# Pooled attention and a top-1 mixture of experts: other key ranges for V's chunks, and low weight halves on another engine

## The chip, the cores and the metric

The kernel runs on one core of a Trainium2 chip. The core has a matrix engine (TensorE, in the profile PE, with its weight loads shown apart as PEld), a vector engine (VectorE, DVE), a scalar engine (ScalarE, ACT), GpSimd (POOL), SyncE (SP), which here only issues transfers, and 16 DMA engines. The metric is the time of the program on the device in microseconds (us), the median of a few runs; lower is better. The profile is of one further execution.

## The reference

Attention over pooled keys and values, and then a mixture of experts in which each token goes to one expert:

```python
# q, k, v: [8 batches, 8 heads, 576 tokens, 64]; pool = 8, so Sp = 72 pooled keys per head
k_p = k.reshape(B, H, Sp, pool, D).mean(axis=3)
v_p = v.reshape(B, H, Sp, pool, D).mean(axis=3)
scores = scale * np.matmul(q, k_p.transpose(0, 1, 3, 2))
attn = softmax(scores)                               # with + 1e-9 in the denominator
attn_out = np.matmul(attn, v_p)
x = attn_out.transpose(0, 2, 1, 3).reshape(4608, 512)
logits = x @ w_gate                                  # 8 experts
e = argmax(logits); gate_w = softmax(logits)[e]
out = gate_w * (relu(x @ w1[e]) @ w2[e])             # w1: 512 x 1024, w2: 1024 x 512 per expert
```

All data are float32.

## The kernel before

There are two stages. The first, up to about 200 us, is attention with the routing of its tokens; the second runs blocks of up to 256 tokens of one expert through that expert's two weight matrices.

**Attention.** The work is cut into 36 *units* of 128 tokens: four full units for each batch, and one unit for each pair of batches that holds the last 64 tokens of both (the *pair units*). One turn of the loop at line 937 does unit i. In each turn it emits, in this order: the pieces of GpSimd's work that are put down for this unit at position "q"; `u_pt(i)`, five transposes of the unit's unnormalised attention weights on TensorE and their copy to SBUF on ScalarE (line 494); half the scores of a later unit (`g_s`, line 468); transposes of later queries (`g_qt`, line 445); row minima on VectorE (`g_min`, line 478) and exponentials on ScalarE (`g_exp`, line 485); `u_pv(i)`, the matmuls with V (line 519, for pair units 514); small steps of the routing of earlier tokens (`fill`); the work put down at "dve3"; the transfers put down at "sp"; another half of scores; and `u_nrm(i)`, which normalises what `u_pv` left (lines 549 to 551). Each engine takes its instructions in this order and waits for the others by semaphores. `put(i, position, f)` is how work is assigned to a unit by hand.

`u_pv` writes to one PSUM tile `po`, of which there is one. So the V matmuls of unit i + 1 wait until line 551 of unit i has read it. Its matmuls are float32, and each is two instructions on TensorE.

**V in chunks.** The 576 pooled keys of a batch (8 heads of 72) lie on 128 partitions as five chunks c. `HS[c]` is the first head that chunk c touches, and `VB` holds for each chunk three masked copies of V, one for each head slot, with 8 columns of the gate's logits and a column of ones, 73 columns in all (`CW`). `SLOTS[c]` says which slots are multiplied. The chunks begin at keys 0, 128, 256, 384 and 512. Heads 0 to 3 lie in one PSUM bank and 4 to 7 in the next, so a chunk across this border takes two matmuls. In all a full unit has six matmuls of 2, 3, 1, 2, 3 and 1 heads: 12 heads, 876 columns.

**Pooling.** Groups of 8 tokens of K and V are added up by three additions of halves. For batch 0 VectorE does it (`pool_now`), and for the others GpSimd (`pool`, lines 327, 329 and 330), one K or V in two units, from `POOLAT[b]` on; batch 7 ends in unit 23. There are three buffers `kv`, so a transfer of K or V waits until GpSimd has read the one three before it. `masked` (line 406) writes pooled V into `VB`.

**K's half.** `v_act` appends to `moves` a copy of 64 partitions of pooled K from one half of `BD` to the other; line 968 issues it on SyncE's queue, where all loads are issued too.

**Weights.** The first expert's weights (float32) are loaded by four transfers of 1 MB (`wload`) and split each into two float16 halves: the high half on ScalarE (`wsplit`, "h", line 111), then the low half, what is left over. There are eight parts j. The low half of j = 0, 2, 5, 6, 7 is made on GpSimd by two instructions on a whole part (lines 118 and 119, "p"), and of j = 1, 3, 4 on VectorE in four pieces of 256 columns, in four units one after another (`lsplit`, line 804). `on_beat` makes such an instruction of GpSimd wait for the latest reciprocal of line 550.

**Routing.** After each group of four units a chain of small VectorE instructions (lines 593 to 649, among them 600, 606 and 615) finds each token's expert; TensorE ranks tokens (line 624) when line 615 is done, and GpSimd scatters the rows to DRAM (line 653). In units 33 to 35 TensorE already begins with the first expert's block (`up_early`, lines 924 to 926), and GpSimd prepares its tokens in unit 30 (`first_block`, lines 838 and 839).

Of the kernel before, what the change touches and what calls it, by code (L numbers as in the profile page):

```python
# [17 lines left out]
POOL = 8  # L18
# [5 lines left out]
UPAT = (33, 34, 35)  # L24
HS = (0, 1, 3, 5, 5)
SLOTS = ((0, 2), (0, 3), (0, 3), (0, 3), (2, 3))


@with_exitstack
def kernel(  # L30
# [110 lines left out]
    for c in range(5):  # L141
        nc.gpsimd.iota(rows[:, c, :], pattern=[[-KP, 3]], base=128 * c - KP * HS[c], channel_multiplier=1,
                       allow_small_or_imprecise_dtypes=True)
# [97 lines left out]
    def load_kv(b, src):  # L241
        dst = kv[(2 * b + (src is vf)) % 3]
        nc.sync.dma_start(dst[0:64, 4, :], src[b, 512:576, :])
        step = 2 if b == 0 else 4
        for c in range(4 - step, -1, -step):
            nc.sync.dma_start(dst[:, c:c + step, :],
                              src[b, 128 * c:128 * (c + step), :].rearrange("(c p) x -> p c x", p=128))
# [24 lines left out]
    nc.vector.memset(kv[0][64:128, 4, :], 0.0)  # L272
    for i in range(1, 3):
        nc.gpsimd.memset(kv[i][64:128, 4, :], 0.0)
    nc.vector.memset(BD[0], 0.0)
# [55 lines left out]

    def pool_now(src, dst, part):
        p1 = pbig[:, 0:1280].rearrange("p (c x) -> p c x", c=5)
        p2 = pbig[:, 1280:1920].rearrange("p (c x) -> p c x", c=5)
        c = (slice(2, 5), slice(0, 2))[part]
        nc.vector.tensor_tensor(p1[:, c], src[:, c, 0:4 * D], src[:, c, 4 * D:], op=OP.add)
        nc.vector.tensor_tensor(p2[:, c], p1[:, c, 0:2 * D], p1[:, c, 2 * D:], op=OP.add)
        nc.vector.tensor_tensor(dst[:, c], p2[:, c, 0:D], p2[:, c, D:], op=OP.add)
# [58 lines left out]
    def u_dve(b):  # L397
        pm, vp = KVS.pop(("pu", b)), KVS.pop(("vp", b))

        def gates():  # L400
            nc.vector.tensor_tensor(VB[b % 3][:, :, :, D:D + E], pm[:, 0:120].rearrange("p (c s e) -> p c s e", s=3, e=E),
                                    mk[:, :, :, None].to_broadcast([128, 5, 3, E]), op=OP.mult)

        def masked(lo, hi):
            n = hi - lo
            nc.vector.tensor_tensor(VB[b % 3][:, lo:hi, :, 0:D], vp[:, lo:hi, None, :].to_broadcast([128, n, 3, D]),
                                    mk[:, lo:hi, :, None].to_broadcast([128, n, 3, D]), op=OP.mult)
            if hi == 5:
# [79 lines left out]
    def u_pt(i):  # L488
        p = pbuf[i % 4]
        pp = psA.tile([128, 1024], F32, name="pp")  # L490
        for c in range(5):
            nc.tensor.transpose(pp[:, c * 128:(c + 1) * 128], p[:, c * 128:(c + 1) * 128], ident)  # L492
        pt = work.tile([128, 640], F32, name="pt")
        nc.scalar.activation(pt, pp[:, 0:640], AF.Copy)  # L494
        PP_[i] = pt

    def u_pv(i):
        b, r = units[i]
        a = PP_.pop(i)
        assert {b, b + (r is None)} <= laid and all(m[2] > b + (r is None) for m in moves)  # L500
        po = psA.tile([128, 2, 512], F32, name="po")
        PO_[i] = po
        first = {}
        for c in range(5):
            h0, hend = HS[c] + SLOTS[c][0], HS[c] + SLOTS[c][1]
            while h0 < hend:
                half = h0 // 4
                h1 = min(hend, 4 * half + 4)
                sl = slice(h0 - HS[c], h1 - HS[c])
                cols = slice((h0 - 4 * half) * CW, (h1 - 4 * half) * CW)  # L510
                st = first.get(half, True)
                if r is None:
                    for s in range(2):
                        nc.tensor.matmul(po[64 * s:64 * s + 64, half, cols],
                                         a[:, c * 128 + 64 * s:c * 128 + 64 * s + 64],
                                         VB[(b + s) % 3][:, c, sl, 0:CW], start=st, stop=False,
                                         skip_group_check=True)
                else:
                    nc.tensor.matmul(po[:, half, cols], a[:, c * 128:(c + 1) * 128],  # L519
                                     VB[b % 3][:, c, sl, 0:CW], start=st, stop=False, skip_group_check=True)  # L520
                first[half] = False
                h0 = h1

# [12 lines left out]
    def u_nrm(i, also=None):  # L536
        gidx, u = GOF[i]
        gs = bounds[gidx][1]
        if u == 0:
            drain(gidx - 2)  # L540
            flush(99, gidx - (3 if i < 30 else 2))
            X = XR[:, i % 12:i % 12 + gs, :]
            L = work.tile([128, 6, E], F32, name="L", bufs=2)
            GRP[gidx] = (X, L)
        X, L = GRP[gidx]
        po = PO_.pop(i)
        pv = po[:, :, 0:4 * CW].rearrange("p a (h x) -> p a h x", x=CW)
        ri = work.tile([128, 2, 4, 1], F32, name="ri")
        nc.vector.tensor_scalar(ri, pv[:, :, :, 72:73], 1e-9, POOL / SX, op0=OP.add, op1=OP.mult)
        beat.append(nc.vector.reciprocal(ri, ri))  # L550
        nc.vector.tensor_tensor(X[:, u, 0:RW].rearrange("p (a h x) -> p a h x", a=2, h=4), pv[:, :, :, 0:HW],  # L551
                                ri.to_broadcast([128, 2, 4, HW]), op=OP.mult)
        if also:
            also()
# [154 lines left out]
    src, kp = pooled("kp", 0)  # L709
    pool_now(src, kp, 0)  # L710
    pool_now(src, kp, 1)
    g_qt(0, 0)
# [8 lines left out]
    src, vp = pooled("vp", 0)  # L721
    pool_now(src, vp, 0)
    now(0, 0)
    pool_now(src, vp, 1)
    g_s(0, 1)
# [49 lines left out]
    for g in range(NPAIR):  # L775
# [16 lines left out]
        if g + 1 < NPAIR:  # L792
            put(u0 + 1, "sp", load_q, e + 2)
            put(u0 + 6, "sp", load_q, o + 2)
            put(u0 + 5, "sp", load_ql, g + 1)
    for j, at in enumerate((9, 14, 24, 22)):
        put(at, "sp", wload, 0, (2 * j, 2 * j + 2))
# [7 lines left out]

    for j, at in enumerate((12, 13, 18, 17, 26, 27, 23, 28)):
        put(at, "act2", wsplit, 0, j, "h")
    for j, at in ((0, 24), (2, 25), (6, 26), (5, 28), (7, 29)):
        put(at, "q", wsplit, 0, j, "p", 0, on_beat)
    for j, at in ((1, 15), (3, 23), (4, 27)):  # L810
        for x in range(4):
# [125 lines left out]
    for i in range(NU):  # L937
# [362 lines left out]
```

## Time and profile before

| what | value |
|---|---|
| median of 3 runs | 611.68 us (611.6 to 613.2) |
| the profiled execution, its own time | 610.65 us |
| its span, from first to last instruction | 608.6 us |
| TensorE busy | 581.4 us (96%) |
| VectorE, ScalarE, GpSimd busy | 304.0, 274.8, 263.1 us |
| mean granted clock of TensorE | 0.991 |
| moved by DMA | 107.10 MB |

The span is 2.05 us shorter than the time of the same execution, and that time is 1.03 us below the median of the runs. Busy time counts instructions that are in an engine; the time in brackets behind an instruction is how long its engine stood idle before it, with what ended the wait. On TensorE instructions overlap, so the distance between starts tells more than a duration. The clock is a share of 2.4 GHz; 0.5 is 1.2 GHz.

### The profile page before, as it was taken

To read this page: it belongs to the slowest core of one execution; us is meant where nothing else is said; L and a number is where in the kernel's file an instruction comes from. 1 tells how busy PE (TensorE), PEld (TensorE's weight loads), DVE (VectorE), ACT (ScalarE), POOL (GpSimd) and SP (SyncE) were. 2 spreads that over 40 slices of the span, in tenths; PEclk is the share of its full clock that TensorE was granted. 3 is DMA by queue.
4 is the path that set the end of the run, shared out by engine and by line. 5 is a ranking of instruction groups with operands and counts; after the bars stand their busy time and mean duration, and the time that the engine had idled before them with its cause. 6 is when DMAs were issued, how large, how long until landed. Compare 5 with 4: busy or idle time off the path is not lost. (4 is left out here: it accounts for less than half of the span.)

```text
span 608.6 us, 15118 instructions
## 1 busy us (share of the span) xinstructions
PE 581.4 (96%) x4391; PEld 436.9 (72%) x4392; DVE 304.0 (50%) x618; ACT 274.8 (45%) x620; POOL 263.1 (43%) x476
## 2 busy tenths in 40 slices
PE   6799999999799999999999999999999999999994
PEld 4699999898799467667756766757767567667672
DVE  5357778879865645214623212273123722183683
ACT  1577687877662245214522212272222722172671
POOL 5675888789964514202321121313222221214265
PEclk9999999999799999999999999999999999999998
DMA  9996789973345795985592143328543192318320
GB/s 246 301 318 203 259 249 328 326 233 136 117 114 191 192 350 128 406 237 108 136 323 66 54 108 83 83 55 284 153 108 81 35 355 81 102 34 291 90 59 11
DMA packets 96256, 107.10 MB, mean 176 GB/s; under 512 B 54366, under 2 KB 64606, under 8 KB 96224
## 3 DMA queue, kind: packets, MB, share of 16 engines
q1 hardware_dynamic: 89584, 85.72, 48.9%
q0 software_dynamic: 6640, 20.99, 9.1%
q8 instruction: 16, 0.26, 0.2%
q14 instruction: 16, 0.13, 0.1%
HBM read 72.99 MB, written 23.37 MB: 158 GB/s over the span
## 5 line engine op out<-in xcount | busy, mean ns | idle before, releaser
L998 PEld LDWEIGHTS <-bd 128*128 128x128 f16 x936 | 91.2, 98 | 105.8 <-DVE bd L992 0.9
L992 DVE SCALAR_TENSOR_TENSOR bd<-ps,bd 128x512 f16<-128x512 f32 (+1 forms) x44 | 27.5, 630 | 144.1 <-ACT bd L988 144.0
L1208 POOL TENSOR_TENSOR spacer<-ql,iG 1x1 f32<-1x1 f32 x44 | 18.6, 422 | 162.8 <-ACT ql L1204 153.0
L485 ACT ACTIVATE both<-ps,nmx 128x72 f32<-128x72 f32 x288 | 69.8, 347 | 7.1 <-DVE nmx L478 7.0
L519 PE MATMUL po<-vb,pt 128*128 128x146 f32 (+2 forms) x384 | 61.1, 308 | 1.5 <-DVE both L551 1.3
L519 PEld LDWEIGHTS po<-vb,pt 128*128 128x128 f32 x384 | 57.5, 192 | 4.0 <-issue 1.7
L998 PE MATMUL po<-w,bd 128*128 128x512 f16 x264 | 59.2, 379 | 0.0
L998 PE MATMUL po<-kv,bd 128*128 128x512 f16 x264 | 58.8, 379 | 0.0
L1209 POOL DMA_INDIRECT out_dram<-ql,iG x44 | 47.1, 1071 | 22.0 <-issue 20.6
L988 ACT ACTIVATE bd<-ps 128x512 f16<-128x512 f32 (+1 forms) x44 | 23.8, 547 | 69.1 <-PE L924 55.5
L468 PE MATMUL ps<-bd,qT 128*128 128x144 f32 x256 | 47.5, 313 | 2.1 <-ACT bd L720 1.4
L998 PE MATMUL pq<-kv,bd 128*128 128x512 f16 x216 | 48.1, 379 | 0.0
L653 POOL DMA_INDIRECT x_by_expert<-both,rpos x36 | 36.3, 1009 | 23.1 <-DVE both L649 10.1
L327 POOL TENSOR_TENSOR st<-kv 128x1280 f32<-128x1280 f32 x14 | 40.6, 2897 | 12.1 <-DVE ri L550 9.6
L926 PE MATMUL ps<-kv,qt 128*128 128x256 f16 (+1 forms) x176 | 44.8, 263 | 0.9 <-DVE qt L113 0.9
L924 PE MATMUL ps<-kv,w 128*128 128x256 f16 (+1 forms) x176 | 43.1, 258 | 1.9 <-ACT kv L111 1.5
L924 PE MATMUL ps<-kv,qt 128*128 128x256 f16 (+1 forms) x176 | 44.8, 263 | 0.0
L925 PE MATMUL ps<-kv,qt 128*128 128x256 f16 (+1 forms) x176 | 44.8, 263 | 0.0
L494 ACT ACTIVATE pt<-pp 128x640 f32<-128x640 f32 x36 | 25.5, 708 | 41.8 <-PE pp L492 41.8
L926 PE MATMUL ps<-kv,w 128*128 128x256 f16 (+1 forms) x176 | 43.1, 258 | 0.0
L925 PE MATMUL ps<-kv,w 128*128 128x256 f16 (+1 forms) x176 | 43.1, 258 | 0.0
L998 PE MATMUL pq<-w,bd 128*128 128x512 f16 x192 | 42.7, 379 | 0.0
(236 smaller groups left out, 1284.4 us busy)
## 6 DMA issues: line engine op xcount, KB each, us to landing
st<-in_moe_w_dram SPq DMA_DIRECT2D x8, 2048.0 KB, 13.7
both<-in_moe_w_dram SPq DMA_DIRECT2D x6, 2048.0 KB, 12.7
vb<-x_by_expert SPq DMA_DIRECT2D x16, 578.0 KB, 4.4
kv<-in_k_dram SPq DMA_DIRECT2D x7, 1024.0 KB, 9.0
kv<-in_v_dram SPq DMA_DIRECT2D x7, 1024.0 KB, 11.4
qt<-in_q_dram SPq DMA_DIRECT2D x6, 1024.0 KB, 11.5
st<-in_moe_w_dram SPq DMA_DIRECT2D x4, 1024.0 KB, 7.1
qt<-in_q_dram SPq DMA_DIRECT2D x4, 512.0 KB, 7.1
```

The source lines that it names most:

```text
L327: on_beat(nc.gpsimd.tensor_tensor(t1, src[:, :, 0:4 * D], src[:, :, 4 * D:], op=OP.add))
L468: nc.tensor.matmul(ps[:, x * 2 * KP:(x + 1) * 2 * KP], t[:, h, :], BD[b % 3][:, :, h, :], start=True, stop=True)
L485: nc.scalar.activation(p[:, h * KP:(h + 1) * KP], ps[:, x * KP:(x + 1) * KP], AF.Exp, bias=nmx[:, x:x + 1], scale=-1.0)
L494: nc.scalar.activation(pt, pp[:, 0:640], AF.Copy)
L519: nc.tensor.matmul(po[:, half, cols], a[:, c * 128:(c + 1) * 128], VB[b % 3][:, c, sl, 0:CW], start=st, stop=False, skip_group_check=True)
L653: st = nc.gpsimd.indirect_dma_start(out=xs, out_offset=bass.IndirectOffsetOnAxis(ap=Z["pos"][:, u:u + 1], axis=0), in_=X[:, u, :], in_offs ...
L924: nc.tensor.matmul(dst, wh, xT[:, d, 0:n], start=(d == 0), stop=False)
L925: nc.tensor.matmul(dst, wh, xT[:, DC + d, 0:n], start=False, stop=False)
L926: nc.tensor.matmul(dst, wl, xT[:, d, 0:n], start=False, stop=(d == DC - 1))
L992: V.scalar_tensor_tensor(l, p, 0.0, h, op0=OP.max, op1=OP.subtract)
L998: nc.tensor.matmul(y, hT[x][:, f, 128 * j:128 * j + 128], W2[s][z][:, f, :], start=(half == x == z == f == 0), stop=(half == z == 1 and f ...
L1209: st = nc.gpsimd.indirect_dma_start(out=out, out_offset=bass.IndirectOffsetOnAxis(ap=iG[:, j:j + 1], axis=0), in_=ys[j], in_offset=None, b ...
```

## The change

- V's chunks begin at keys 0, 128, 216, 344 and 472 (`VK`). Keys 216 to 255 lie in two chunks, and the slots that are multiplied leave them out of one. The five chunks multiply 2, 2, 2, 3 and 2 heads, and heads 0 to 2 lie at the end of one PSUM bank and 3 to 7 at the start of the next (`LEFT`), so no chunk crosses the border: five matmuls, 11 heads, 803 columns. `u_nrm` reads the eight heads as one run. `masked` leaves out the third slot of chunks 0 to 2.
- V is loaded by three transfers, 256, 256 and 104 rows of 2 KB, 616 rows in place of 576. For batch 0 the two large ones come first, and `pool_now` of V takes chunks 0 and 1 first and then 2 to 4. The part of V's first buffer that is not loaded is zeroed on GpSimd ahead of the loads.
- All eight low halves are made on VectorE in pieces of 256 columns: 32 pieces in place of 12, and none on GpSimd. The second, third and fourth loads of the weights and the high halves from j = 2 on are put down for other units.
- K's half is copied by a transfer that is issued on ScalarE's queue.

```diff
-HS = (0, 1, 3, 5, 5)
-SLOTS = ((0, 2), (0, 3), (0, 3), (0, 3), (2, 3))
+VK = (0, 128, 216, 344, 472)
+HS = (0, 1, 3, 4, 5)
+SLOTS = ((0, 2), (0, 2), (0, 2), (0, 3), (1, 3))
+LEFT = 3
...
     def load_kv(b, src):
         dst = kv[(2 * b + (src is vf)) % 3]
+        if src is vf:
+            for c in (0, 2):
+                nc.sync.dma_start(dst[:, c:c + 2, :],
+                                  src[b, VK[c]:VK[c] + 256, :].rearrange("(c p) x -> p c x", p=128))
+            nc.sync.dma_start(dst[0:S - VK[4], 4, :], src[b, VK[4]:S, :])
+            return
...
+    nc.gpsimd.memset(kv[1][96:128, 4, :], 0.0)
     load_kv(0, kf)
...
-    for i in range(1, 3):
-        nc.gpsimd.memset(kv[i][64:128, 4, :], 0.0)
+    nc.gpsimd.memset(kv[2][64:128, 4, :], 0.0)
...
         def masked(lo, hi):
-            n = hi - lo
-            nc.vector.tensor_tensor(VB[b % 3][:, lo:hi, :, 0:D], vp[:, lo:hi, None, :].to_broadcast([128, n, 3, D]),
-                                    mk[:, lo:hi, :, None].to_broadcast([128, n, 3, D]), op=OP.mult)
+            n, m = hi - lo, max(SLOTS[c][1] for c in range(lo, hi))
+            nc.vector.tensor_tensor(VB[b % 3][:, lo:hi, 0:m, 0:D], vp[:, lo:hi, None, :].to_broadcast([128, n, m, D]),
+                                    mk[:, lo:hi, 0:m, None].to_broadcast([128, n, m, D]), op=OP.mult)
...
-            nc.tensor.transpose(pp[:, c * 128:(c + 1) * 128], p[:, c * 128:(c + 1) * 128], ident)
+            nc.tensor.transpose(pp[:, c * 128:(c + 1) * 128], p[:, VK[c]:VK[c] + 128], ident)
...
-        po = psA.tile([128, 2, 512], F32, name="po")
-        PO_[i] = po
...
+        po = psA.tile([128, 2, 512], F32, name="po").rearrange("p a x -> p (a x)")
+        o0 = 512 - LEFT * CW
+        PO_[i] = po[:, o0:o0 + H * CW]
         for c in range(5):
...
+            sl = slice(*SLOTS[c])
+            h = HS[c] + SLOTS[c][0]
+            cols = slice(o0 + h * CW, o0 + (HS[c] + SLOTS[c][1]) * CW)
...
+                nc.tensor.matmul(po[:, cols], a[:, c * 128:(c + 1) * 128], VB[b % 3][:, c, sl, 0:CW],
+                                 start=h in (0, LEFT), stop=False, skip_group_check=True)
...
-    pool_now(src, vp, 0)
+    pool_now(src, vp, slice(0, 2))
     now(0, 0)
-    pool_now(src, vp, 1)
+    pool_now(src, vp, slice(2, 5))
...
-    for j, at in enumerate((9, 14, 24, 22)):
+    for j, at in enumerate((9, 20, 25, 22)):
         put(at, "sp", wload, 0, (2 * j, 2 * j + 2))
...
-    for j, at in enumerate((12, 13, 18, 17, 26, 27, 23, 28)):
+    for j, at in enumerate((12, 13, 22, 23, 28, 29, 25, 26)):
         put(at, "act2", wsplit, 0, j, "h")
-    for j, at in ((0, 24), (2, 25), (6, 26), (5, 28), (7, 29)):
-        put(at, "q", wsplit, 0, j, "p", 0, on_beat)
-    for j, at in ((1, 15), (3, 23), (4, 27)):
+    for j, at in enumerate((13, 17, 23, 24, 30, 32, 27, 28)):
         for x in range(4):
             put(at + x, "dve3", lsplit, j, x, 4)
...
         for _ in range(len(moves)):
-            nc.sync.dma_start(*moves.pop(0)[:2])
+            nc.scalar.dma_start(*moves.pop(0)[:2])
```

## Rows read from the trace of the kernel before

**Rows 1.** Busy time by window: PE, PEld, DVE, ACT, POOL, then clock, DMA share.
```profile
75.00:100.00 25.00, 24.91 (x202) 23.61 (x201) 18.77 (x49) 20.36 (x68) 21.66 (x21) 1.00 0.90 271
...
125.00:150.00 25.00, 23.76 (x204) 22.10 (x203) 21.64 (x55) 18.72 (x66) 21.98 (x21) 1.00 0.64 211
150.00:175.00 25.00, 21.64 (x148) 20.84 (x147) 19.39 (x44) 16.32 (x51) 22.95 (x30) 0.86 0.35 103
```

**Rows 2.** TensorE's timeline, 140 to 200 us; columns: start, duration, instruction, count, idle before.
```profile
141.41 0.19 PE L624 MATMUL pq<-oh,before 128*128 128x32 f16 x1 [1.24 <-DVE oh L615]
...
156.42 1.91 PE L519 MATMUL po<-vb,pt 128*128 128x146 f32 x12
161.69 0.18 PE L624 MATMUL pq<-oh,before 128*128 128x32 f16 x1 [3.36 <-DVE oh L615]
...
165.81 2.79 PE L519 MATMUL po<-vb,pt 128*128 128x146 f32 x12
...
170.54 1.91 PE L519 MATMUL po<-vb,pt 128*128 128x146 f32 x12
172.28 0.70 PE L468 MATMUL ps<-bd,qT 128*128 128x144 f32 x4
...
174.39 1.91 PE L519 MATMUL po<-vb,pt 128*128 128x146 f32 x12
```

**Rows 3.** PV matmuls of line 519 by shape; last row: all shapes together.
```profile
L519 PE MATMUL po<-vb,pt 128*128 128x219 f32 x128 | 34.5, 351 | 0.0
...
L519 PE MATMUL po<-vb,pt 128*128 128x146 f32 x128 | 30.9, 323 | 1.5 <-DVE both L551 1.3 <-ACT pt L494 0.2
...
L519 PE MATMUL po<-vb,pt 128*128 128x73 f32 x128 | 21.7, 250 | 0.0
...
L519 PE MATMUL po<-vb,pt 128*128 128x146 f32 (+2 forms) x384 | 61.1, 308 | 1.5 <-DVE both L551 1.3
```

**Rows 4.** VectorE's timeline, 156 to 180 us.
```profile
157.11 1.89 DVE L600 TENSOR_TENSOR ra<-L,rm 128x32 f32<-128x32 f32 x1
159.03 2.16 DVE L606 SCALAR_TENSOR_TENSOR req<-ra,down 128x32 f32<-128x32 f32 x1
...
179.13 0.19 DVE L606 SCALAR_TENSOR_TENSOR req<-ra,down 128x32 f32<-128x32 f32 x1
```

**Rows 5.** GpSimd's timeline, 110 to 160 us.
```profile
110.98 2.89 POOL L327 TENSOR_TENSOR st<-kv 128x1280 f32<-128x1280 f32 x1 [2.22 <-DMA kv<-in_v_dram]
...
157.03 1.91 POOL L118 TENSOR_TENSOR kv<-st,swc 128x1024 f32<-128x1024 f32 x1
159.02 2.12 POOL L119 TENSOR_TENSOR w<-kv,w 128x1024 f16<-128x1024 f32 x1
```

**Rows 6.** VectorE's timeline at 111 us.
```profile
111.22 3.73 DVE L406 TENSOR_TENSOR vb<-vp,mk 128x576 f32<-128x576 f32 x2
```

**Rows 7.** TensorE's waits between 25 and 200 us: total, times, longest.
```profile
PE po L519 <- DVE both L551: 1.3, 1, 1.3
```

**Rows 8.** SyncE's queue: timeline at 86 us.
```profile
86.41 0.49 SPq L968 DMA_DIRECT2D bd<-bd  x1
86.99 0.55 SPq L243 DMA_DIRECT2D kv<-in_k_dram  x1
```

**Rows 9.** SyncE's waits up to 200 us: total, times, longest.
```profile
SPq L968 <- ACT vT L387: 56.0, 6, 13.6
```

**Rows 10.** VectorE's low-half pieces on line 804: duration min, median, max.
```profile
L804 DVE SCALAR_TENSOR_TENSOR w<-st,w x12: 395/419/2190, 97.9 to 170.6; 128x256 f16<-128x256 f32 x12
```

**Rows 11.** VectorE's waits between 25 and 200 us.
```profile
DVE ri L549 <- PE po L519: 26.2, 23, 3.2
```

**Rows 12.** ScalarE's waits between 25 and 200 us.
```profile
ACT pt L494 <- PE pp L492: 41.8, 32, 4.1
```

**Rows 13.** The first 40 us, all engines in order of time.
```profile
11.00 0.96 DVE L336 TENSOR_TENSOR st<-kv 128x768 f32<-128x768 f32 x1 [1.61 <-DMA kv<-in_v_dram]
...
20.28 0.66 PE L371 MATMUL pq<-ident,vp 128*128 128x128 f32 x2 [1.06 <-DVE vp L338]
```

More of the change, by code (lines that the diff above doesn't have):

```diff
@@ L141 @@
     for c in range(5):
-        nc.gpsimd.iota(rows[:, c, :], pattern=[[-KP, 3]], base=128 * c - KP * HS[c], channel_multiplier=1,
+        nc.gpsimd.iota(rows[:, c, :], pattern=[[-KP, 3]], base=VK[c] - KP * HS[c], channel_multiplier=1,
                        allow_small_or_imprecise_dtypes=True)
@@ L330, in pool, with pool_now @@
             nc.gpsimd.tensor_tensor(dst, t2[:, :, 0:D], t2[:, :, D:], op=OP.add)
-    def pool_now(src, dst, part):
+    def pool_now(src, dst, c):
         p1 = pbig[:, 0:1280].rearrange("p (c x) -> p c x", c=5)
         p2 = pbig[:, 1280:1920].rearrange("p (c x) -> p c x", c=5)
-        c = (slice(2, 5), slice(0, 2))[part]
         nc.vector.tensor_tensor(p1[:, c], src[:, c, 0:4 * D], src[:, c, 4 * D:], op=OP.add)
@@ L500, in u_pv @@
         assert {b, b + (r is None)} <= laid and all(m[2] > b + (r is None) for m in moves)
-        po = psA.tile([128, 2, 512], F32, name="po")
-        PO_[i] = po
-        first = {}
+        po = psA.tile([128, 2, 512], F32, name="po").rearrange("p a x -> p (a x)")
+        o0 = 512 - LEFT * CW
+        PO_[i] = po[:, o0:o0 + H * CW]
         for c in range(5):
[L505 to L522, printed above, removed]
+            sl = slice(*SLOTS[c])
+            h = HS[c] + SLOTS[c][0]
+            cols = slice(o0 + h * CW, o0 + (HS[c] + SLOTS[c][1]) * CW)
+            if r is None:
+                for s in range(2):
+                    nc.tensor.matmul(po[64 * s:64 * s + 64, cols], a[:, c * 128 + 64 * s:c * 128 + 64 * s + 64],
+                                     VB[(b + s) % 3][:, c, sl, 0:CW], start=h in (0, LEFT), stop=False,
+                                     skip_group_check=True)
+            else:
+                nc.tensor.matmul(po[:, cols], a[:, c * 128:(c + 1) * 128], VB[b % 3][:, c, sl, 0:CW],
+                                 start=h in (0, LEFT), stop=False, skip_group_check=True)
     GRP = {}
@@ L545, in u_nrm @@
         X, L = GRP[gidx]
[L546 to L549, printed above, removed]
+        pv = PO_.pop(i).rearrange("p (h x) -> p h x", x=CW)
+        ri = work.tile([128, H, 1], F32, name="ri")
+        nc.vector.tensor_scalar(ri, pv[:, :, 72:73], 1e-9, POOL / SX, op0=OP.add, op1=OP.mult)
         beat.append(nc.vector.reciprocal(ri, ri))
-        nc.vector.tensor_tensor(X[:, u, 0:RW].rearrange("p (a h x) -> p a h x", a=2, h=4), pv[:, :, :, 0:HW],
-                                ri.to_broadcast([128, 2, 4, HW]), op=OP.mult)
+        nc.vector.tensor_tensor(X[:, u, 0:RW].rearrange("p (h x) -> p h x", x=HW), pv[:, :, 0:HW],
+                                ri.to_broadcast([128, H, HW]), op=OP.mult)
         if also:
@@ L709 @@
     src, kp = pooled("kp", 0)
-    pool_now(src, kp, 0)
-    pool_now(src, kp, 1)
+    pool_now(src, kp, slice(2, 5))
+    pool_now(src, kp, slice(0, 2))
     g_qt(0, 0)
```

## The prediction

> **What bounds the kernel now.** I read the busy times by window first. Between 75 and 150 us TensorE is busy 23.8 to 24.9 us of 25 [rows 1], more than any other engine; GpSimd has 21.7 to 22 us, VectorE and ScalarE 18.7 to 21.6. Between 150 and 175 us TensorE falls to 21.64 us and its granted clock to 0.86. So attention runs at TensorE's pace, with one hole. TensorE's timeline shows the pace and the hole. From the first V matmul of unit 30 (170.54) to that of unit 31 (174.39) it is 3.85 us, and no idle time stands between [rows 2]. The hole is ahead of line 624, which waited 3.36 us for line 615 of VectorE; in the unit after it the V matmuls take 2.79 us in place of 1.91 [rows 2]. The same wait costs 1.24 us at 141 us [rows 2], and the V matmuls wait 1.3 us once for line 551 [rows 7].
>
> Why VectorE is late stands in its own timeline. Line 606 works on 32 columns and takes 0.19 us at 179.13, where nothing is beside it. At 157.11 line 600, as small, takes 1.89 us, and line 606 behind it 2.16 [rows 4]. In just these stretches GpSimd runs lines 118 and 119, the low half of a part, 157.03 for 1.91 us and 159.02 for 2.12 [rows 5], and each of the two instructions ends with the one beside it. At 111.22 the two masks of line 406 take 3.73 us, beside a pooling addition of 2.89 us that had waited 2.22 us for V from DRAM [rows 5, 6].
>
> **The change, part by part.** My sum is made against the profiled execution, 610.65 us, whose span is 608.6. The median of the runs is 611.68, so 1.03 us are added at the end.
>
> *V's chunks.* Before, the V matmuls of a full unit are 12 instructions in three shapes, four of each: 128 of each shape are the 32 full units [rows 3]. After, eight have 146 columns, two 219, and none 73. The mean durations are 351, 323 and 250 ns [rows 3]; 2 x 0.351 less, 4 x 0.250 less and 4 x 0.323 more make 0.41 us. They overlap: the three rows add up to 87.1 us and all of them together cover 61.1 us [rows 3], so I count 0.41 x 61.1 / 87.1 = 0.29 us for a unit. The bounds: from the first V matmul to what comes next it is 1.74 us (170.54 to 172.28) [rows 2]; by columns the saving is 73/876 of it, 0.145 us, by instructions 2/12, 0.29 us. I take the upper end because an instruction of 73 columns costs 250 ns, not a half of 323: it has half the columns and nearly the same time. 32 x 0.29 = 9.2 us. For the four pair units no row of mine gives a price; between nothing and 0.29 I take 0.2, so 0.8. Together 10.0 us, between 5.2 (36 x 0.145) and 10.4. All of this is on the path as long as TensorE sets the pace. What is late next is the copy on ScalarE ahead of the V matmuls, and VectorE's line 551; both are below.
>
> *Low halves off GpSimd.* Lines 118 and 119 go away, five of each. So the wait of 1.24 us goes, and the hole: from the V matmuls of unit 28 (156.42) to those of unit 30 (170.54) it is 14.12 us [rows 2] where two units at 3.85 make 7.70; of the 6.4 between I count 6.3, the ranking staying. About half of it is the wait and the rest is the clock: (1 - 0.86) x 25 / 0.5 is 7.0 us at 1.2 GHz, after the wait [rows 1, 2]. 1.24 + 6.3 = 7.5 us. A loss is excluded here; a smaller gain is what the next part is about.
>
> *Low halves on VectorE.* 20 more pieces at the median of 0.419 us [rows 10] are 8.4 us for VectorE. What hides them is its waiting for the V matmuls, 26.2 us in 23 waits, 1.1 us each [rows 11]. In units 13 to 20 there is one piece in each, and that is covered. In units 24 to 33 there are 21 pieces where there were 7, so 14 x 0.419 = 5.9 us in ten units, three of them in unit 30, where `first_block` has GpSimd work as well. Uncovered, they delay lines 549 to 551, and the V matmuls of the next unit wait for these. Bounds 0 and 5.9; since a unit also gets shorter by 0.29 I take 2.0.
>
> *K's half on ScalarE's queue.* SyncE stood 56.0 us at line 968, up to 13.6 us at a time [rows 9], and a load of K was issued right behind one at 86.99 [rows 8]. After, the loads of K, V, q and the weights queued behind it start when their buffers are free. With the second weight load moved from unit 14 to 20 this should bring V in time, and take away the 1.3 us at line 551 [rows 7]; between 0 and 1.3 I take it whole. On ScalarE the issue costs 0.49 us [rows 8], six times, 2.9 us; it waits for nothing but ScalarE's own copies ahead of it. Behind it are the high half of a part and the next unit's copy of line 494. ScalarE waited 41.8 us in 32 waits for that unit's transposes [rows 12], 1.3 us each, and 1.0 when a unit is 0.29 shorter. So it is hidden alone; where a high half falls in the same unit or in a short one it isn't. Between 0 and 2.9 I take 0.5.
>
> *GpSimd.* It loses ten instructions of about 2 us [rows 5], all after pooling. In the pooling units it has as much to do as before in less time: 21.98 of 25 us [rows 1] becomes some 23.6. That fits, barely; 0 to 2 us, I take 0.5.
>
> *Transfers.* 40 more rows of 2 KB for each of eight batches are 0.66 MB; at 271 GB/s (75 to 100 us) [rows 1] 2.4 us of all queues. The DMA share there is 0.90, so they fit; 0 to 2.4, I take 0. Issuing three transfers in place of two costs SyncE about one half microsecond, which the wait at line 968 now leaves free.
>
> *The start.* Batch 0's second half of V is three chunks in place of two. The first addition of three chunks takes 0.96 us [rows 13], so one is 0.32; the second and third have half and a quarter of the columns, 0.56 in all. TensorE waits for it at 20.28 [rows 13]. I take 0.4, between 0 and 0.56. The narrower masks give VectorE something back, which I count at nothing: it goes into its waits.
>
> Sum: -10.0 - 7.5 - 1.3 + 2.0 + 0.5 + 0.5 + 0.4 = -15.4. That is 595.25 for a profiled execution, 596.3 for the median of runs. The second stage begins when attention ends, and every load and count in it hangs on that end, so I let it move as a whole.
>
> **The rivals.** *Only the columns count.* If a V matmul is as long as its columns, 5.2 us are saved in place of 10.0: 601.1 us. For it: the whole stream is 61.1 us for 32 x 1752 columns [rows 3], which is about 1 ns a column. Against it: the 250 ns of 73 columns.
>
> *VectorE becomes the bound.* In units 24 to 33 all 5.9 us are uncovered, and one wait is long enough for the clock to fall as at 161 us, where what came on top of the wait was 6.4 - 3.36, about 3 us [rows 2]. Then 596.3 + 3.9 + 3.0 = 603.2. For it: VectorE is busy 21.64 of 25 us already between 125 and 150 [rows 1]. Against it: the long instructions in that stretch were GpSimd's doing.
>
> *Transfers become the bound.* K and V come at the pace of before until unit 23, so 24 x 0.29 = 7.0 us of the gain are not had and 2.4 us are added: 605.7. For it: a DMA share of 0.90 and the late V at 110.98 [rows 1, 5]. Against it: that V was issued behind a blocked SyncE.
>
> *Slower: pieces are caught by pooling.* Nine pieces now lie in units 13 to 20 and 23, beside GpSimd's first additions of 2.9 us [rows 5]. A piece that is caught can last as long as the addition: 2.5 us more, less the 1.1 us that VectorE waits anyway, a stall of 1.4; with a fall of the clock 3 us on top, 4.4 each. The gain of 15.4 is eaten at three and a half pieces: from the fourth on the kernel is slower (four: 613.9). Against it: of the 12 pieces of before four lie in pooling units 15 to 18, the median is 0.419 and the longest 2.19 [rows 10]. The Trainium skill speaks for it: "SBUF — State Buffer", section "Who interferes with whom", says that a VectorE instruction with two SBUF inputs and a GpSimd instruction that reads SBUF shut each other out for the whole instruction, whichever started first. By that rule, the trace agrees in lines 600 and 606, and a piece of line 804, with two SBUF inputs, is of the same kind; it leaves open how often they meet.
>
> **How the numbers follow.** The forecast has 0.58, the columns alone 0.13, VectorE 0.12, transfers 0.09, caught pieces 0.08. The likeliest case's own range is 592.5 (611.68 less all of 10.4 + 8.8) to 601, where the uncovered costs go to their upper ends together. The time said is 596.3. The range 591.5 to 604 takes in the first three cases and leaves out some 0.17 to 0.2. A measurement of this kernel tells 0.3% (1.8 us) from no change. Faster by more: 0.90; within: 0.04; slower: 0.06, the last two from caught pieces, and a share from two costs together.
>
> **What would show it.** The V matmuls of a full unit are ten instructions, and from the first to what follows it is about 1.45 us; a plain unit takes 3.56. Lines 118 and 119 are gone, 600 and 606 stay near 0.2 us from unit 24 on, TensorE doesn't wait for line 615, and the clock is 1.00 through attention. The last line 551 comes some 15 us earlier. Wrong would be: V matmuls at 1.6 us (columns alone); waits of the V matmuls for line 551 in units 24 to 33 (VectorE); GpSimd waiting for K or V at line 327 (transfers); pieces of line 804 over 1 us in units 13 to 23 (caught).

## The result, and the profile after

The changed kernel takes 607.32 us in the median of 12 runs (603.1 to 611.0), against 611.8 for 12 runs of the kernel before beside it: a ratio of 0.9915, 95% interval 0.9894 to 0.9937. That is 5.2 us less (3.9 to 6.5) where 15.4 were forecast, and 3.3 us above the upper end of the range. The profiled execution took 605.55 us, its span is 603.8.

Lines have moved a little: 549 to 551 are now 548 to 550, 600, 606 and 615 are 599, 605 and 614, 624 is 623, 519 is 521, 468 is 475, 804 is 803, 968 is 965, the pooling's first addition 327 is 335, and `pool_now` has lines 343 to 345 (336 to 338 before). The gate that comes up below is an addition of one element, `spacer <- vp[0:1, 0, 0:1]`, line 742 (743 before): GpSimd has it ahead of its first pooling, so it starts that when VectorE has written this element of batch 0's pooled V.

Busy time by window, the columns of [rows 1]: the clock is 1.00, and from 150 us on GpSimd has half the work. TensorE is still not busy throughout from 150 us on; what is left of the hole comes below.

```profile
75.00:100.00 25.00, 23.97 (x196) 22.52 (x197) 21.56 (x57) 20.11 (x68) 21.07 (x19) 1.00 0.95 301
125.00:150.00 25.00, 24.37 (x207) 22.38 (x205) 19.45 (x62) 21.84 (x69) 17.39 (x24) 1.00 0.67 219
150.00:175.00 25.00, 22.23 (x176) 20.08 (x175) 22.47 (x68) 19.27 (x64) 11.38 (x22) 1.00 0.32 94
```

TensorE's timeline in two plain units, and its V matmuls by shape:

```profile
63.22 0.65 PE L475 MATMUL ps<-bd,qT 128*128 128x144 f32 x4
...
65.27 1.64 PE L521 MATMUL po<-vb,pt 128*128 128x146 f32 x10
66.75 0.65 PE L475 MATMUL ps<-bd,qT 128*128 128x144 f32 x4
```

```profile
L521 PE MATMUL po<-vb,pt 128*128 128x146 f32 x256 | 44.8, 296 | 1.0 <-ACT pt L501 0.6 <-DVE both L550 0.4
L521 PE MATMUL po<-vb,pt 128*128 128x219 f32 x64 | 17.1, 347 | 0.0
```

The V matmuls are ten instructions without 73 columns, 1.48 us (65.27 to 66.75) in place of 1.74 [rows 2]. From one unit's scores to the next's it is 3.53 us (63.22 to 66.75) in place of 3.85 [rows 2], so 0.32 are saved in a plain unit, 0.26 of them in the V matmuls; the forecast was 0.29. The saving is there; what is lost again shows in TensorE's waits between 25 and 186 us, beside [rows 7]:

```profile
PE pq L378 <- DVE vp L345: 5.0, 1, 5.0
PE pq L623 <- DVE oh L614: 4.7, 5, 1.8
```

The first of them stands in the timeline of the start, all engines, which answers to [rows 13]. Ahead of it is the gate's line in the kernel before:

```profile
20.22 0.18 POOL L743 TENSOR_TENSOR spacer<-vp,zf 1x1 f32<-1x1 f32 x1 [10.87 <-DVE vp L338]
```

```profile
12.51 0.18 POOL L742 TENSOR_TENSOR spacer<-vp,zf 1x1 f32<-1x1 f32 x1 [3.08 <-DVE vp L345]
19.14 0.95 DVE L343 TENSOR_TENSOR st<-kv 128x768 f32<-128x768 f32 x1
...
19.31 3.52 POOL L335 TENSOR_TENSOR st<-kv 128x1280 f32<-128x1280 f32 x1 [6.62 <-DMA kv<-in_k_dram]
...
20.12 3.12 DVE L344 TENSOR_TENSOR st<-st 128x384 f32<-128x384 f32 x1
...
23.28 1.57 DVE L345 TENSOR_TENSOR vp<-st 128x192 f32<-128x192 f32 x1
...
24.90 0.47 PE L378 MATMUL pq<-ident,vp 128*128 128x128 f32 x1 [5.00 <-DVE vp L345]
```

VectorE now pools chunks 0 and 1 first. The gate looks at chunk 0 and opens at 12.51 us; in the kernel before that element was in the second half. So GpSimd starts its addition when K has come, at 19.31 us, and that is beside VectorE's second half. Line 344 takes 3.12 us there and ends 0.4 us behind the addition, and line 345 takes 1.57 beside GpSimd's second one; in e1_gate below, with GpSimd not yet started, they take 0.56 and 0.36. TensorE gets V at 24.90 where it got it at 20.28 [rows 13].

The four smaller of the five waits at line 623 look like this one, in unit 16:

```profile
102.27 2.91 POOL L335 TENSOR_TENSOR st<-kv 128x1280 f32<-128x1280 f32 x1
...
103.81 1.44 DVE L599 TENSOR_TENSOR ra<-L,rm 128x32 f32<-128x32 f32 x1
...
105.98 0.19 PE L623 MATMUL pq<-oh,before 128*128 128x32 f16 x1 [0.77 <-DVE oh L614]
```

Line 599 is held until the pooling ends (105.25 and 105.18 us), and TensorE, whose V matmuls are shorter now, waits for the one-hot behind it. In the kernel before the same line was held as well (units 8 and 16 are shown), but TensorE still had V matmuls then: its wait at line 624 was 0.17 us in unit 8 and nothing in unit 16, and its two long ones lie elsewhere [rows 2]:

```profile
67.74 0.96 DVE L600 TENSOR_TENSOR ra<-L,rm 128x32 f32<-128x32 f32 x1
...
102.55 0.84 DVE L600 TENSOR_TENSOR ra<-L,rm 128x32 f32<-128x32 f32 x1
```

The line is also held longer than before: 1.55, 1.69 and 1.44 us in units 8, 12 and 16, in place of 0.96, 1.06 and 0.84. In unit 16 it begins 2.6 us behind the last line 548 (549 before) in both kernels, but the pooling begins 1.06 us behind that line in place of 0.50, so more of the pooling is still to come. There the longer hold (0.60 us) makes more of the wait of 0.77 than the shorter V matmuls (0.26) do.

The fifth wait is in unit 28. With lines 118 and 119 gone, GpSimd comes earlier to the split of the first block (835 and 836), and that meets the ranking chain:

```profile
154.68 1.18 POOL L836 TENSOR_TENSOR bd<-vb,bd 128x512 f16<-128x512 f32 x1
154.88 1.03 DVE L605 SCALAR_TENSOR_TENSOR req<-ra,down 128x32 f32<-128x32 f32 x1
...
155.83 1.03 POOL L835 TENSOR_TENSOR bd<-vb,zf 128x512 f16<-128x512 f32 x1
...
156.17 0.74 DVE L614 TENSOR_TENSOR oh<-req,rm 128x32 f16<-128x32 f32 x1
...
156.96 0.18 PE L623 MATMUL pq<-oh,before 128*128 128x32 f16 x1 [1.78 <-DVE oh L614]
```

### The profile page after: what moved, and what is told of

It is laid out like the page before. It is cut to its first block, busy times and chain, and to the rows that moved or that the text cites. A ratio compares the mean times of both kernels' runs of the same rounds, so it can differ in the third digit from the quotient of the medians.

```text
span 603.8 us, 14968 instructions
## 1 busy us (share of the span) xinstructions
PE 569.6 (94%) x4311; PEld 422.2 (70%) x4312; DVE 304.7 (50%) x638; ACT 274.5 (45%) x620; POOL 246.3 (41%) x466
## 5 line engine op out<-in xcount | busy, mean ns | idle before, releaser
L521 PE MATMUL po<-vb,pt 128*128 128x146 f32 (+1 forms) x320 | 51.6, 306 | 1.0 <-ACT pt L501 0.6
L521 PEld LDWEIGHTS po<-vb,pt 128*128 128x128 f32 x320 | 45.4, 188 | 3.6 <-ACT pt L501 2.5
L475 PE MATMUL ps<-bd,qT 128*128 128x144 f32 x256 | 45.0, 302 | 2.1 <-ACT bd L719 1.4
L485 DVE TENSOR_REDUCE nmx<-ps 128x4 f32<-128x288 f32 x72 | 32.2, 451 | 15.4 <-PE ps L475 14.0
```

Of the source, the lines that this page charges most:

```text
L475: nc.tensor.matmul(ps[:, x * 2 * KP:(x + 1) * 2 * KP], t[:, h, :], BD[b % 3][:, :, h, :], start=True, stop=True)
L485: nc.vector.tensor_reduce(nmx, ps[:, 0:4 * KP].rearrange("p (h x) -> p h x", x=KP), axis=AX.X, op=OP.min)
L521: nc.tensor.matmul(po[:, cols], a[:, c * 128:(c + 1) * 128], VB[b % 3][:, c, sl, 0:CW], start=h in (0, LEFT), stop=False, skip_group_check ...
```

## The experiments

Each ratio is against runs of the kernel before on the same chip; a difference in us is the ratio's times 611.68. The theory after the result: three small things eat most of the two thirds of the gain that are missing, the gate, line 599 beside the pooling, and the earlier split. The rivals stand in each expectation.

**e1_gate, and the parts of the change alone.** The gate reads an element of the half that VectorE now writes second:

```diff
-    nc.gpsimd.tensor_tensor(spacer[:, 0:1], vp[0:1, 0, 0:1], zf[0:1], op=OP.add)
+    nc.gpsimd.tensor_tensor(spacer[:, 0:1], vp[0:1, 4, 0:1], zf[0:1], op=OP.add)
```

> The changed kernel with one address changed: the small GpSimd instruction that holds back the pooling of batch 1's K reads pooled V of chunk 4 (written last) in place of chunk 0 (now written first). Theory (the gate opens too early, so GpSimd's pooling shuts out VectorE's second half of V at the start): line 548 of unit 0 starts at 34.0 to 34.6 us in place of 37.7, TensorE's wait of 5.0 us for pooled V falls to about 1.5, and the whole is 3 to 4 us shorter than the changed kernel. Rival (V's last chunks land late, whatever the gate does): the wait stays at 4 to 5 us and the time stays within 1 us.

602.11 us, ratio 0.9833 (0.9807 to 0.986). The start of its timeline:

```profile
19.38 0.56 DVE L344 TENSOR_TENSOR st<-st 128x384 f32<-128x384 f32 x1
...
20.39 0.48 PE L378 MATMUL pq<-ident,vp 128*128 128x128 f32 x1 [1.23 <-DVE vp L345]
```

One index gives back 5.0 us by the ratios, 2.9 to 7.1 with both intervals. Line 344 takes 0.56 us where it took 3.12. Between the two profiles it is a little less: unit 0's line 548 begins at 33.78 us in place of 37.72, and unit 34's at 175.97 in place of 180.12, so 3.9 to 4.2 us.

**e2_chunks** is the kernel before with V's chunks, and with that gate; against e1_gate it undoes the rest:

```diff
-    for j, at in enumerate((9, 20, 25, 22)):
+    for j, at in enumerate((9, 14, 24, 22)):
...
-    for j, at in enumerate((12, 13, 22, 23, 28, 29, 25, 26)):
+    for j, at in enumerate((12, 13, 18, 17, 26, 27, 23, 28)):
         put(at, "act2", wsplit, 0, j, "h")
-    for j, at in enumerate((13, 17, 23, 24, 30, 32, 27, 28)):
+    for j, at in ((0, 24), (2, 25), (6, 26), (5, 28), (7, 29)):
+        put(at, "q", wsplit, 0, j, "p", 0, on_beat)
+    for j, at in ((1, 15), (3, 23), (4, 27)):
...
-            nc.scalar.dma_start(*moves.pop(0)[:2])
+            nc.sync.dma_start(*moves.pop(0)[:2])
```

> The kernel before with V's chunks alone (other keys, three loads, five matmuls, the narrower masks), and the gate on chunk 4. Theory (the V matmuls do save 0.32 us a unit, and about 1 us is given back in each of the units 8, 12, 16 and 20 where the ranking then waits for VectorE): 36 x 0.32 less 4 x 0.9 is 8 us faster than before, waits for line 614 four to six times. Rival (only columns count): 5 us faster, and a plain unit of 3.70 us. Rival (nothing is given back): 11 us or more.

606.73 us, ratio 0.9917 (0.9888 to 0.9947): 5.1 us less, a half of the term of 10.0. TensorE's waits for the one-hot, first in the kernel before (1.24 and 3.36 [rows 2] are two of the three), then in e2_chunks:

```profile
PE pq L624 <- DVE oh L615: 4.8, 3, 3.4
PE pq L623 <- DVE oh L614: 8.2, 6, 2.8
```

8.2 less 4.8 us: 3.4 us of the saving turn into waits of TensorE for VectorE. 3.0 of them are in units 8, 12, 16 and 20 (0.94, 1.03, 0.69 and 0.53 us, where there was 0.17 in all).

**e3_low** is the kernel before with the low halves on VectorE, and the loads and high halves put down for the units of the change:

```diff
...
-    for j, at in ((0, 24), (2, 25), (6, 26), (5, 28), (7, 29)):
-        put(at, "q", wsplit, 0, j, "p", 0, on_beat)
-    for j, at in ((1, 15), (3, 23), (4, 27)):
+    for j, at in enumerate((13, 17, 23, 24, 30, 32, 27, 28)):
...
```

> The kernel before with the low halves alone: all on VectorE, with the changed places of loads and high halves. Theory (the hole at 140 to 168 us was GpSimd's doing): 5 to 7.5 us faster than before, granted clock 1.00 through attention. Rival (VectorE is too full in units 24 to 33): less than 3 us, with the V matmuls waiting for line 551 there.

604.77 us, ratio 0.9888 (0.9861 to 0.9916): 6.9 us less. At line 624 two waits are left, of 1.2 us together:

```profile
PE pq L624 <- DVE oh L615: 1.2, 2, 1.0
```

**e4_moves** is the kernel before with K's half on ScalarE's queue:

```diff
-            nc.sync.dma_start(*moves.pop(0)[:2])
+            nc.scalar.dma_start(*moves.pop(0)[:2])
```

> The kernel before with K's half moved on ScalarE's queue alone. Forecast's term: 0.5 to 1.3 us faster, the wait of 1.3 us at line 551 near 115 us gone. Rival (V of batch 6 is late for another reason): within 0.5 us of before, the wait still there. Rival (ScalarE pays for it): 0.5 to 3 us slower.

612.52 us, ratio 1.0013 (0.9993 to 1.0034): no change. The three parts alone make -5.1 - 6.9 + 0.8 = -11.2 us; all of them with the gate put right make -10.2. Within their intervals they add up, and the 5 us that the changed kernel lacks of this sum are the gate.

**f4_gate_early** tries the gate from the other side: the kernel before, whose first half holds chunk 4, with the gate on chunk 4 (the diff is that of e1_gate).

> The kernel before with one thing changed: the gate ahead of GpSimd's first pooling reads chunk 4 in place of chunk 0, and chunk 4 is there written by VectorE's first half. Theory (the lost 5 us at the start come of a gate that opens while VectorE still pools the second half): GpSimd's first addition starts beside VectorE's second half and stretches it, TensorE's first values block starts later by 1.5 to 4 us and the time rises by as much, to between 613.3 and 616 us; less than the 5 us of the changed kernel, as the second half is the smaller one here. Rival (the loss in the changed kernel comes of the order of the chunks itself, not of the gate): the time stays within 0.5 us of before.

615.09 us, ratio 1.0068 (1.0046 to 1.0089): 4.2 us more (2.8 to 5.4), where I gave 1.5 to 4. The start of its timeline, with line 336 at 3.26 us where it took 0.68, and TensorE's wait at 5.39 where it was 1.06 [rows 13]:

```profile
18.82 2.88 POOL L327 TENSOR_TENSOR st<-kv 128x1280 f32<-128x1280 f32 x1 [5.39 <-DMA kv<-in_k_dram]
18.98 3.26 DVE L336 TENSOR_TENSOR st<-kv 128x512 f32<-128x512 f32 x1
...
24.92 0.66 PE L371 MATMUL pq<-ident,vp 128*128 128x128 f32 x2 [5.39 <-DVE vp L338]
```

The order of the chunks is the old one here, so the gate alone is the cause.

**f1_rank** is e1_gate with the ranking of groups 1 to 4 one slot later:

```diff
-    def fill_pe():
-        if fillers and fillers[0][1]:
+    def fill_pe(late={1, 2, 3, 4}):
+        if fillers and fillers[0][1] and not (fillers[0][0] in late and not late.discard(fillers[0][0])):
```

> The changed kernel with the gate on chunk 4, and TensorE's ranking products of the second to fifth group (units 8, 12, 16, 20) issued one slot later, after the next scores instead of right behind the values. Theory (part of what the shorter values blocks save is given back where TensorE waits for VectorE's one-hot of line 614): the waits of 0.94, 0.90, 0.76 and 0.62 us at these four units go, nothing takes their place, and the time falls by 2 to 3 us against the gate's kernel, to about 599.5 us; those units come down from some 4.9 to some 4.1 us. Rival (VectorE's own chain sets the length of a ranking unit): the wait moves to the next line that needs VectorE, the values' line behind the normalising of line 550 or the ranking itself one slot on, and the time is within 0.8 us of the gate's kernel.

602.92 us, ratio 0.9871 (0.9848 to 0.9895). The theory's saving didn't come; by the ratios it is 2.3 us slower than e1_gate, more than the rival gave too; the two are on different chips, and their intervals overlap a little. Its timeline in unit 16:

```profile
100.08 2.91 POOL L335 TENSOR_TENSOR st<-kv 128x1280 f32<-128x1280 f32 x1
...
100.44 2.60 DVE L599 TENSOR_TENSOR ra<-L,rm 128x32 f32<-128x32 f32 x1
...
105.31 0.97 PE L517 MATMUL po<-vb,pt 128*64 128x146 f32 x12 [1.18 <-DVE both L550]
```

The wait at the ranking is gone, but the shorter units bring line 599 to the beginning of the pooling. It is held for 2.60 us, and TensorE waits for line 550 in its place. So moving the ranking doesn't remove the loss; in these units the wait goes on to the next line that needs VectorE.

**f2_split** is e1_gate with the split of the first block on the beat:

```diff
-            nc.gpsimd.tensor_tensor(h[:, j], x[:, j], zf[:, :, None].to_broadcast([128, H, D]), op=OP.add)
+            on_beat(nc.gpsimd.tensor_tensor(h[:, j], x[:, j], zf[:, :, None].to_broadcast([128, H, D]), op=OP.add))
```

> The changed kernel with the gate on chunk 4, and GpSimd's split of the first block of tokens (lines 835 and 836) held until VectorE has passed line 549 of the unit in which it is issued, some 7 us later than it now runs. Theory (the earlier split collides with VectorE's lines 605, 614 and 803 in unit 28): the wait of about 1 us in unit 28 and the two of 0.4 us behind it go, and the time falls by 1 to 2 us, to about 601 us. Rival (the wait in unit 28 is ScalarE's or the ranking chain's own): no change within 0.5 us, and unit 28 still waits about 1 us.

599.44 us, ratio 0.9814 (0.979 to 0.9839). In unit 28 nothing is held any more, and the split comes at 156.91:

```profile
151.74 0.19 DVE L605 SCALAR_TENSOR_TENSOR req<-ra,down 128x32 f32<-128x32 f32 x1
...
152.18 0.19 DVE L614 TENSOR_TENSOR oh<-req,rm 128x32 f16<-128x32 f32 x1
...
152.43 0.18 PE L623 MATMUL pq<-oh,before 128*128 128x32 f16 x1 [0.23 <-DVE oh L614]
...
156.91 1.03 POOL L835 TENSOR_TENSOR bd<-vb,zf 128x512 f16<-128x512 f32 x1 [11.12 <-ACT both L492]
```

By the ratios this edit is worth 1.2 us (0.9833 to 0.9814), with intervals that overlap; two more pairs of the same edit, each on one chip, have 2.1 (f1_rank, f3_both) and 1.0 (g2_pool, g1_pool_split).

**f3_both** has the two edits together.

> Both of the edits before it in one kernel: the later ranking and the later split, on top of the gate on chunk 4. If the two waits are separate, as the theory has it, their savings add: 598 to 599.5 us. If both only move VectorE's lateness along, it stays at 601 to 602 us.

601.17 us, ratio 0.9836 (0.9811 to 0.9861): 1.3 us above f2_split and 2.1 below f1_rank, on one chip. The signs are those of the single edits, the later ranking costs and the later split saves, though each difference is within the intervals.

**g1_pool_split, g2_pool, g3_pool_before** hold the first addition of K's pooling until the one-hot is written, in units 8, 12, 16 and 20, on f2_split, on e1_gate and on the kernel before:

```diff
-            V.tensor_tensor(Z["oh"], Z["eq"][:, 0:gs], Z["m2"][:, 0:gs].to_broadcast(sh), op=OP.is_equal)
+            (beat.append if 1 <= gidx <= 4 else id)(V.tensor_tensor(Z["oh"], Z["eq"][:, 0:gs], Z["m2"][:, 0:gs].to_broadcast(sh), op=OP.is_equal))
...
-                        put(POOLAT[b] + x + y, "q", f, b, y)
+                        put(POOLAT[b] + x + y, "dve3" if b > 3 and x == y == 0 else "q", f, b, y)
```

> The changed kernel with the gate on chunk 4, the later split of the first block, and GpSimd's first addition of K's pooling for batches 4 to 7 (line 335, in units 8, 12, 16, 20) held until VectorE has written the one-hot of line 614 in that unit, so that it can't run beside line 599. Theory (line 599, the difference of the logits and their maximum, waits out the pooling, and that is where TensorE's wait for the one-hot comes from): line 599 falls from 1.3 to 1.4 us to 0.2 us in these four units, TensorE's waits at line 623 of 0.4 to 0.8 us go, and the time falls by 1.5 to 3 us against the kernel with the later split, to 597 to 598 us. Rival (the collision goes on to the next unit's VectorE lines, as it did when the ranking was moved): the units behind, 9, 13, 17 and 21, grow by as much, and the time stays at 599 to 600 us.

> The same held pooling on the changed kernel with the gate on chunk 4, the split of the first block where the change has it. Theory: 599.5 to 600.5 us, 1.5 to 2.5 us below the gate's kernel, and line 599 at 0.2 us in units 8, 12, 16 and 20. Rival: no change from the gate's 602.1 us within 0.8 us.

> The same held pooling on the kernel before, where the values blocks are still the longer ones. Theory (there the stretched subtraction, line 600, lies behind the longer values block and costs TensorE nothing): line 600 falls from about 1 us to 0.2 us in units 8, 12, 16 and 20, and the time stays within 0.8 us of before. Rival (the collision already cost the kernel before as much, so that the shorter values blocks gave nothing back there): it falls by 1.5 to 2.5 us.

605.14 us, ratio 0.9901 (0.9873 to 0.9929); 606.31, 0.9917 (0.9899 to 0.9934); 614.44, 1.0046 (1.0029 to 1.0063). All three are slower than what they start from, by 5.3, 5.1 and 2.8 us, which is outside what either theory gave. g2_pool's timeline in units 8 and 9, and TensorE's waits:

```profile
67.30 0.18 DVE L599 TENSOR_TENSOR ra<-L,rm 128x32 f32<-128x32 f32 x1
...
68.24 2.89 POOL L335 TENSOR_TENSOR st<-kv 128x1280 f32<-128x1280 f32 x1 [2.86 <-DVE oh L614]
68.58 0.19 PE L623 MATMUL pq<-oh,before 128*128 128x32 f16 x1
...
71.88 3.58 DVE L413 TENSOR_TENSOR vb<-vp,mk 128x384 f32<-128x384 f32 x2
```

```profile
PE po L521 <- DVE both L550: 6.2, 5, 2.3
PE pq L623 <- DVE oh L614: 1.8, 2, 1.6
```

Line 599 takes 0.18 us and TensorE doesn't wait at line 623 in these units: that the pooling beside line 599 makes the wait there is shown. But the rest of the pooling now falls on the masks of line 413, two instructions that took 1.02 us together in e1_gate and take 3.58 here, and TensorE waits longer for line 550. The rival had the place right and its size too small. As in f1_rank, the collision is moved and not removed.

**h1_pieces, h2_split_again.** The first addition of each pooling in three instructions, on f2_split; and f2_split once more on the same chip.

```diff
-            on_beat(nc.gpsimd.tensor_tensor(t1, src[:, :, 0:4 * D], src[:, :, 4 * D:], op=OP.add))
+            for c in (slice(0, 2), slice(2, 4), slice(4, 5)): on_beat(nc.gpsimd.tensor_tensor(t1[:, c], src[:, c, 0:4 * D], src[:, c, 4 * D:], op=OP.add))
```

> The changed kernel with the gate on chunk 4 and the later split, and GpSimd's first addition of each pooling (line 335, one instruction of 2.9 us) issued as three, of two, two and one chunks. Theory (VectorE's line 599 waits for the end of the GpSimd instruction that runs, not for GpSimd's work as such): VectorE gets in between two pieces, line 599 falls from 1.05 to 1.43 us to 0.3 to 0.8 us in units 8, 12, 16 and 20, nothing is moved to other lines, and the time falls by 1 to 2 us, to 597.5 to 598.5 us. Rival (VectorE stays locked out while GpSimd has a queue of such work): line 599 keeps its length, and the time stays within 0.8 us of the kernel with the later split, or rises by some 0.5 us for the added instructions.

> The kernel with the gate on chunk 4 and the later split once more, unchanged, on the chip of the run before it, to set the pieces against it: 599.4 us as before, between 598 and 601 us.

600.68 us, ratio 0.984 (0.982 to 0.9861), against 598.99, 0.9816 (0.9792 to 0.984). The pieces are 1.5 us slower by the ratios, with intervals that overlap. Their timeline in units 8 and 20:

```profile
65.28 3.18 POOL L335 TENSOR_TENSOR st<-kv 128x512 f32<-128x512 f32 x3
...
67.18 1.34 DVE L599 TENSOR_TENSOR ra<-L,rm 128x32 f32<-128x32 f32 x1
...
117.32 3.19 POOL L335 TENSOR_TENSOR st<-kv 128x512 f32<-128x512 f32 x3
118.74 1.15 DVE L599 TENSOR_TENSOR ra<-L,rm 128x32 f32<-128x32 f32 x1
119.93 0.64 DVE L605 SCALAR_TENSOR_TENSOR req<-ra,down 128x32 f32<-128x32 f32 x1
```

In unit 8 line 599 ends at 68.52, with the last of the three pieces (65.28 + 3.18 = 68.46); a boundary between two pieces lay within its 1.34 us and didn't let it in. In unit 20 it ends at 119.89, over half a microsecond before the last piece does, and line 605 behind it is held until 120.57. So cutting the instruction didn't reliably shorten the hold.

## Why the prediction was wrong

In terms of the sum:

| term | forecast | measured alone |
|---|---|---|
| V's chunks, with GpSimd's 0.5 | -9.5 | -5.1 (-6.9 to -3.2) |
| low halves, off GpSimd and on VectorE | -5.5 | -6.9 (-8.5 to -5.1) |
| K's half: SyncE unblocked, ScalarE's cost | -0.8 | +0.8 (-0.4 to +2.1) |
| the start | +0.4 | +5.0 (2.9 to 7.1; the changed kernel against e1_gate) |

**The start** is the step that failed outright. It priced VectorE's third chunk and left out who waits for VectorE there. The gate names an element, not a half; when the halves changed places it opened at 12.51 us in place of 20.22, and let GpSimd run beside VectorE. The direction was right, the size was 0.4 us for 5.0. What the term did price came out right: in e1_gate the three additions take 1.87 us where they took 1.39, and TensorE has V at 20.39. The change of the two `pool_now` lines stood in the diff, and the gate stands in the kernel among the lines around them.

**V's chunks**: the price of a plain unit was right, 0.32 us where 0.29 were said. "All of this is on the path as long as TensorE sets the pace" is what failed, and it named only ScalarE's copy and line 551 as late next. Late next was the ranking: units in which line 599 is held by the pooling, at next to no cost while the V matmuls were longer. The hold grew too, because the pooling then begins later in the unit; the term for GpSimd asked whether its work still fits into a shorter unit, and not what it then lies beside. Of the 10.2 us that 32 plain units save at 0.32, 3.4 turn into waits at line 623 when the chunks are changed alone; the 6.8 left lie just inside the interval of e2_chunks (3.2 to 6.9).

**The second stage** did not move as a whole, which the sum took for granted. From the start of unit 35's line 548 (549 before) to the end it is 416.5 to 416.9 us in the profiles of the kernel before, f4_gate_early and g3_pool_before, and 418.3 to 419.3 in those of the changed kernel and of the seven runs from f1_rank on that are built on it. The four runs e1_gate to e4_moves scatter from 415.5 to 421.6. So some 2 us that attention gains seem to be lost behind it. Part is a wait in the second stage at a matmul of line 922, for nothing that the profile shows: 1.26 us at 268.84 in the changed kernel, 0.83 at 262.65 in f2_split, none in the kernel before. Its cause stays open; each is one profile.

**Low halves**: right within the interval. The wait of 1.24 us went, that of 3.36 became 1.04 in e3_low, and the changed kernel's clock stayed at 1.00 through attention. What VectorE's 20 further pieces cost by themselves isn't shown. The 32 pieces, beside [rows 10]:

```profile
L803 DVE SCALAR_TENSOR_TENSOR w<-st,w x32: 394/417/1317, 93.3 to 182.6; 128x256 f16<-128x256 f32 x32
```

In units 13 to 23 one piece is over 1 us (1.16 in unit 23, beside the pooling's second addition), where the rival of caught pieces needed four; the longest, 1.317, is in unit 28, beside line 836. The term on VectorE's pieces looked at `first_block` in unit 30. Its split did collide, but in unit 28, and with the ranking's lines 605 and 614 as well: 1.0 to 2.1 us by three pairs of kernels.

**K's half**: the six issues cost ScalarE 0.468 to 0.548 us each, as was said, and SyncE no longer stands ahead of them (the profile puts two waits of V's loads, 16.2 us, down to these copies, but GpSimd waits for no V). In e4_moves the 1.3 us at line 551 are gone too, but the time is the same. New in its waits are 0.5 us at line 468 for K's half itself to land (0.9 in e1_gate, line 475), and 0.9 at line 468 for ScalarE's copy of line 494, at 59.94 us; the last issue ahead of that is at 52.48, so that it is the price of an issue isn't shown. The two together are about as much as the 1.3 us gained.

**Transfers** didn't become the bound in units 1 to 23: the plain units run at 3.53 us, and behind its first addition GpSimd waits for no K or V at line 335. **Columns alone** is refuted by the 1.48 us of the V matmuls. The last line 550 starts at 185.89 us, the last 551 of the kernel before at 192.11: 6.2 us earlier, where some 15 were said.

One reading of the prediction left out a window: between 100 and 125 us TensorE was busy 23.38 us, GpSimd 20.90 and VectorE 21.60, so not every window had TensorE at 23.8 or more and GpSimd second. No term of the sum uses it.

The rule of the Trainium skill that I put into one rival, "SBUF — State Buffer", "Who interferes with whom", was the right one, at the wrong places. VectorE's instructions with two SBUF inputs are held by a GpSimd instruction that reads SBUF: the trace agrees at the start (line 344, 3.12 against 0.56 us), in the ranking (line 599, 1.44 against 0.18) and in unit 28. I asked it of the pieces that the change adds, and not of VectorE's other such lines, which the change moves against GpSimd's. Two inputs aren't a condition for being held: line 645 has one, and in the changed kernel it takes 1.52 us at 78.41, ending with an addition of GpSimd at 79.9, and 0.16 at 141.75.

One thing is open. In the profile of the changed kernel VectorE's line 548 of the last unit begins at 185.45 us after a wait of 2.47, though TensorE's last V matmuls had ended before 184:

```profile
185.45 0.17 DVE L548 TENSOR_SCALAR ri<-po 128x8 f32<-128x8 f32 x1 [2.47 <-PE ps L923]
```

The profiles of e1_gate, e2_chunks, e3_low and e4_moves, all of one chip, have such a wait too, of 2.10 to 2.33 us; those of f1_rank to h2_split_again, of three other chips, have none over 1 us. TensorE's waits behind it, for the last lines of the routing, are longer with it: at lines 1014 and 1119 1.6 us in the changed kernel and 3.3 in e1_gate, where f2_split has 0.5. Whether it comes with the chip or the kernel, and whether it is in other executions, wasn't tried. So the 1.2 us between e1_gate and f2_split can hold some of it; the other two pairs for the split don't have it on either side.

The best version is f2_split: 599.4 and 599.0 us on two chips, ratio 0.9814 and 0.9816, against 0.9915 for the change as it was.

## What to carry to other kernels

When the order of two halves changes, look for everything that waits for one element of them: a gate that reads a fixed element moves with it, in silence. When TensorE's stream gets shorter, list the units in which another engine's chain was just hidden by it, by that chain's length in the trace and not by its waits, since a hidden chain shows none. And an instruction of GpSimd that is moved, or comes earlier because work ahead of it went away, is to be laid against VectorE's instructions in its new place, those with two SBUF inputs first.

## What the runs showed of the hardware

VectorE doesn't always get in between GpSimd instructions that follow each other closely: in h1_pieces line 599 stayed held past the boundary at 67.75 us in unit 8 and was let in at the one at 119.8 in unit 20.

The granted clock that the profile has for a stretch needn't show in the time. e1_gate and f1_rank have the same instructions up to unit 7. Their windows from 10 to 30 us, the columns of [rows 1], first e1_gate and then f1_rank:

```profile
10.00:20.00 10.00, 7.77 (x28) 4.50 (x26) 3.32 (x7) 3.35 (x8) 0.00 (x0) 1.00 1.00 264
20.00:30.00 10.00, 9.12 (x41) 7.94 (x42) 4.35 (x9) 5.82 (x22) 8.86 (x7) 1.00 1.12 316
```

```profile
10.00:20.00 10.00, 7.78 (x28) 4.50 (x26) 3.31 (x7) 3.37 (x8) 0.00 (x0) 0.50 1.04 274
20.00:30.00 10.00, 9.15 (x40) 7.97 (x41) 4.36 (x9) 5.81 (x22) 8.85 (x7) 0.59 1.12 307
```

The one has a granted clock of 1.00 (2.4 GHz) and the other of 0.50 and 0.59 (1.2 GHz in the first window and most of the second), and TensorE's busy time is the same within 0.03 us; unit 0's line 548 begins at 33.78 us in both. I would have charged half a window's work for it.
